# Queries turned ahead of the wait for the key sums, and the key sums of the first pairs from a ones product, in an attention and expert kernel

## The chip, the cores and the metric

The kernel runs on one core of a Trainium2 chip. The metric is the time of one execution on the device in microseconds. The engines are TensorE (PE in the rows, PEld for its weight loads), VectorE (DVE), ScalarE (ACT), GpSimd (POOL) and the DMA queues; SP is the queue of SyncE. Each engine works through its own instructions in the order of the program, and waits on semaphores for the others.

## What is computed

Multi-query attention over 8 batches, 16 heads, 384 positions and head size 64, with one key and value head per batch; its output, as 3072 rows of 1024, goes through a two-level mixture of 4 x 4 experts. All of it is float32 outside; the expert products run in bf16.

```python
scores = scale * np.matmul(q, k.transpose(0, 1, 3, 2))
attn = np.exp(scores - max) ; attn = attn / (sum(attn) + 1e-09)
x = np.matmul(attn, v)            # rows of 16 heads x 64
g_idx = argmax(x @ w_group) ; e_idx = argmax(xg @ w_expert[g])
out[token] = g_w * e_w * (relu(x @ w1[g, e]) @ w2[g, e])
```

## The kernel before

A batch has 16 x 384 query columns. They are cut into 6 chunks `g` of 2 x 512 columns (two heads' halves of the array at once), and two chunks make a pair `p`. So there are 24 pairs, three to a batch `b` (`r` is the pair's place in its batch). The queries arrive in a layout that VectorE's 32 x 32 turn brings into the form TensorE needs: `prep_q` (`qT`, line 176) for a pair of chunks, `prep_k` (`kT`, line 169) for a batch's keys.

The work of a pair:

- `scores(g, kt)`: for one of three blocks of 128 keys, two float32 matmuls of 64 rows each fill a PSUM tile `s` of 2 x 512 columns (line 185; two such tiles exist); ScalarE's exponential writes `pt` (line 187). No maximum is taken off.
- `pre_add` and `fold_keys`: VectorE adds the three `pt` blocks of a chunk in two steps (`presum`, lines 195 and 199), turns the sum in 32 x 32 blocks (`turn`, line 207) and sums along the row (`fold`, line 211). What is left of the sum over keys, 4 partition groups, a small product does in `invert`: `sm` (line 216), then a reciprocal `rc` (218) and a turn that spreads it over the partitions, `rinv` (220).
- `values(g)`: six matmuls of 64 output rows each into `o` (line 232). There is one buffer of `o`, and the gate's products `gps`, `lps` and `cps` take turns in it.
- `weigh(p)`: VectorE multiplies `o` by `rinv` into `xT` (240), which also frees `o`; GpSimd casts to bf16.

Pairs run one behind another: in step `p` the scores of pair `p` are made, and the values, the reciprocal and `xT` of pair `p - 1`. `manual_schedule` keeps the order in which the code is written. Up to pair 6 (`MOE_AT = 7`; `busy` is false) a step holds attention alone, and in some pairs the gate of the batch before: `gate_a` and `gate_b` at `r == 0` (product `gps`, copy, logits `lps`, arithmetic on VectorE with the exponential `ex`), `gate_c` at `r == 1` (counts `cps`, `cnt` at line 299, the choice of the batch's most used expert, and the DMA of its weights from GpSimd's queue). From pair 7 on, `fill(n)` puts `n` units of expert work (`hps`, line 329, and `yps`, line 338) at fixed places of each step. After the last pair follow the units that are left, and the tokens that went to other experts.

Queries are loaded from SyncE's queue three pairs ahead (`load_q(p + 3)` at the end of step `p`), behind `stats_q` on ScalarE, which reads the same buffer.

## Time and profile before

| | before |
|---|---|
| median of 3 runs | 570.04 us (569.46 to 573.44) |
| the profiled execution | 569.86 us, its span 567.9 us |
| TensorE busy | 496.1 us, 87% of the span |
| VectorE busy | 369.9 us, 65% |
| ScalarE busy | 242.0 us, 43% |
| GpSimd busy | 63.8 us, 11% |
| DMA | 73.06 MB, 129 GB/s on average |
| granted clock of TensorE, mean | 0.947 of full speed |

The span runs from the first to the last instruction. The chain of work that ended last lies on TensorE for 67% of the span and on VectorE for 22%. Busy shares are averages over stretches with different limits: the first pairs, the pairs with expert work, and the tail. The granted clock is given as a share of 2.4 GHz; 0.5 is the lower level, 1.2 GHz. A float32 matmul has two records in the trace, so a count there is twice that in the code.

### The profile page before, as it was taken

How to read it: one execution, taken by the hardware profiler on the slowest of the kernel's cores; microseconds unless marked ns; L12 is line 12 of the kernel's file. 1: busy time of each engine (PE TensorE's matmuls, PEld its weight loads, DVE VectorE, ACT ScalarE, POOL GpSimd, SP SyncE). 2: the span in 40 equal slices, each digit the busy share in tenths (PEclk: the TensorE clock that was granted, in tenths of full speed). 3: DMA queues.
4: the chain of work that ended last, by engine and by line, in shares of the span. 5: the costliest groups of instructions: out<-in, count | busy, mean ns of one | idle time of the engine just before them, and what ended most of it. 6: DMA issues, size and time to landing. Idle time of an engine off the chain costs nothing.

```text
span 567.9 us, 6824 instructions
## 1 busy us (share of the span) xinstructions
PE 496.1 (87%) x2521; PEld 210.1 (37%) x2521; DVE 369.9 (65%) x503; ACT 242.0 (43%) x342; POOL 63.8 (11%) x64
## 2 busy tenths in 40 slices
PE   6758677857979997999899998999899979989992
PEld 4222222313434342433443343434343434454550
DVE  2865776796979848775978496787788567241100
ACT  2434225233536444444634562556355435232331
POOL 0010011111011101110021002010111011010000
PEclk8798788879999998999999998999999989999997
DMA  9450223892359843986199529943697129689990
GB/s 122 44 67 0 38 70 47 136 213 74 59 72 216 213 96 43 199 176 160 39 165 201 171 47 143 208 154 85 99 210 176 46 45 206 176 189 236 237 253 16
DMA packets 148377, 73.06 MB, mean 129 GB/s; under 512 B 122587, under 2 KB 122587, under 8 KB 148336
## 3 DMA queue, kind: packets, MB, share of 16 engines
q0 software_dynamic: 19008, 37.84, 36.8%
q1 hardware_dynamic: 114928, 32.53, 27.1%
q10 hardware_dynamic: 14400, 2.16, 2.1%
q8 instruction: 23, 0.38, 0.3%
q14 instruction: 18, 0.15, 0.1%
HBM read 91.31 MB, written 19.40 MB: 195 GB/s over the span
## 4 chain that ended last, share of the span: by engine, by line
PE 67%; DVE 22%; issue 4%; DMA 2%; ACT 2%; SPq 1%; POOL 0%; DVEq 0%; POOLq 0%; ACTq 0%
PE o L232 23%; PE s L185 19%; PE yps L338 12%; PE hps L329 10%; DVE turn L207 4%; DVE presum L199 4%; DVE qT L176 3%; DVE presum L195 2%; DVE rinv L220 2%; DVE xT L240 2%; DMA out_dram<-y 2%; DVE fold L211 2%; PE gps L252 2%; ACT y L340 1%; DVE oh L278 1%
## 5 line engine op out<-in xcount | busy, mean ns | idle before, releaser
L187 ACT ACTIVATE pt<-s 128x1024 f32<-128x1024 f32 x144 | 140.1, 1020 | 175.0 <-PE s L185 174.9
L185 PE MATMUL s<-qT,kT 64*128 64x512 f32 x576 | 155.0, 659 | 35.6 <-DVE qT L176 17.6
L232 PE MATMUL o<-pt,v 128*64 128x512 f32 x576 | 139.8, 634 | 16.0 <-DVE cnt L299 16.0
L329 PE MATMUL hps<-xbf,w 128*128 128x384 bf16 x512 | 89.3, 326 | 2.2 <-ACT hT L331 0.9
L338 PE MATMUL yps<-w,hT 128*128 128x512 bf16 x384 | 89.5, 379 | 1.3 <-ACT y L340 1.3
L185 PEld LDWEIGHTS s<-qT,kT 64*128 64x128 f32 x576 | 53.7, 199 | 96.9 <-issue 79.6
L232 PEld LDWEIGHTS o<-pt,v 128*64 128x64 f32 x576 | 41.0, 145 | 115.3 <-issue 90.2
L195 DVE TENSOR_TENSOR presum<-pt 128x1024 f32<-128x1024 f32 x48 | 57.8, 1205 | 36.6 <-ACT pt L187 36.4
L241 POOL CAST xbf<-xT 128x1024 bf16<-128x1024 f32 x24 | 40.8, 1699 | 350.7 <-DVE xT L240 350.7
L329 PEld LDWEIGHTS <-w 128*128 128x128 bf16 x512 | 48.5, 99 | 48.1 <-issue 18.5
L207 DVE STREAM_TRANSPOSE turn<-presum 128x1024 f32<-128x1024 f32 x48 | 59.8, 1245 | 1.6
L199 DVE TENSOR_TENSOR presum<-presum,pt 128x1024 f32<-128x1024 f32 x48 | 58.6, 1221 | 2.9 <-DVE presum L195 0.5
L211 DVE TENSOR_REDUCE fold<-turn 128x32 f32<-128x1024 f32 x48 | 58.6, 1220 | 1.6
L218 DVE RECIPROCAL rc<-sm 128x32 f32<-128x32 f32 x24 | 8.6, 358 | 77.4 <-PE sm L216 77.4
L338 PEld LDWEIGHTS <-hT 128*128 128x128 bf16 x384 | 37.0, 100 | 51.9 <-issue 14.1
L340 ACT ACTIVATE y<-yps,gsel 128x512 f32<-128x512 f32 x48 | 32.9, 686 | 54.2 <-PE yps L338 49.3
L331 ACT ACTIVATE hT<-hps 128x384 bf16<-128x384 f32 x64 | 31.3, 490 | 40.2 <-PE hps L329 32.9
L176 DVE STREAM_TRANSPOSE qT<-qraw 128x1024 f32<-128x1024 f32 (+1 forms) x25 | 29.7, 1191 | 3.6 <-DMA qraw<-in_q_dram 3.6
L155 ACT ACTIVATE junk<-qraw 128x1024 bf16<-128x1024 f32 x24 | 25.2, 1052 | 14.5 <-DMA k<-in_k_dram 14.4
L220 DVE STREAM_TRANSPOSE rinv<-rc 128x1024 f32<-128x1024 f32 x24 | 29.9, 1245 | 0.8
L240 DVE TENSOR_TENSOR xT<-o,rinv 128x1024 f32<-128x1024 f32 x24 | 29.4, 1224 | 1.3
L93 POOL DMA_DIRECT2D w<-in_moe_w_dram x18 | 12.6, 706 | 101.3 <-DVE gsel L317 76.7
(123 smaller groups left out, 161.1 us busy)
## 6 DMA issues: line engine op xcount, KB each, us to landing
w<-in_moe_w_dram POOLq DMA_DIRECT2D x18, 1024.0 KB, 13.3
w<-in_moe_w_dram POOLq DMA_DIRECT2D x9, 2048.0 KB, 23.7
qraw<-in_q_dram SPq DMA_DIRECT2D x96, 128.0 KB, 3.8
out_dram<-y SPq DMA_DIRECT2D x48, 256.0 KB, 3.4
x_bf<-xbf SPq DMA_DIRECT2D x8, 768.0 KB, 3.4
k<-in_k_dram ACTq DMA_DIRECT2D x28, 48.0 KB, 2.2
v<-in_v_dram ACTq DMA_DIRECT2D x8, 96.0 KB, 2.6
xe<-x_bf SPq DMA_DIRECT2D x1, 768.0 KB, 9.5
```

The lines of the kernel that those rows point to most:

```text
L176: nc.vector.transpose(out=t[:, i * w:(i + 1) * w], in_=src[:, i * w:(i + 1) * w])
L185: nc.tensor.matmul(out=ps[:, par, :], lhsT=kT[b][r, kt * P:(kt + 1) * P], rhs=qT[g][r, :], start=True, stop=True)
L187: nc.scalar.activation(out=t[:], in_=ps[:], func=ACTF.Exp, scale=scale)
L195: nc.vector.tensor_add(out=t[:], in0=pt[g, 0][:], in1=pt[g, 1][:])
L199: nc.vector.tensor_add(out=t[:], in0=t[:], in1=pt[g, 2][:])
L207: nc.vector.transpose(out=t[:], in_=presum[g][:].rearrange("p a n -> p (a n)"))
L211: nc.vector.reduce_sum(out=fold[p][:, ch, :], in_=t[:].rearrange("p (b i) -> p b i", i=32), axis=AX)
L220: nc.vector.transpose(out=t[:].rearrange("p (b i) -> p b i", i=32), in_=rc[:].unsqueeze(2).to_broadcast([P, 32, 32]))
L232: nc.tensor.matmul(out=o_ps[p][64 * par:64 * par + 64, ch, :], lhsT=v_sb[b][:, kt, :], rhs=pt[g, kt][:, par, :], start=(kt == 0), stop=(kt ...
L241: nc.gpsimd.tensor_copy(out=xbf[b][:, cs], in_=xT[b][:, cs])
L329: nc.tensor.matmul(out=ps[:, 0:S], lhsT=w1[:, ko, fc * P:(fc + 1) * P], rhs=xb[:, ko * S:(ko + 1) * S], start=(ko == 0), stop=(ko == KO - 1))
L338: nc.tensor.matmul(out=ps[:], lhsT=state["h"][:, fo, st * P:(st + 1) * P], rhs=w2[:, fo, nh * CW:(nh + 1) * CW], start=(fo == 0), stop=(fo ...
```

## The change

Four things are changed.

- `prep_q(p + 1)` and `prep_k(b + 1)` are issued right after the first key addition of step `p`, ahead of `invert(p - 1)`. Before, they stood behind the first chunk's fold.
- For pairs 0 to 6, the turn and fold of the key sums on VectorE are gone. `sum_keys` puts four float32 matmuls (`kss`) with a block of ones of 32 columns on TensorE, one for each half of each chunk, at four column positions of one PSUM tile; VectorE turns that tile once (`krow`, 512 columns), and `invert` picks one column of each 32-block with four small matmuls instead of two. `presum` has three buffers instead of one.
- Two constants are built at the start (`ones32`, `selq`).
- With expert work, `gate_c` is issued ahead of the second chunk's additions and fold, instead of behind them and two units.

The diff, without a last hunk that gives three buffers to a tile of the fallback path:

```diff
@@ -135,6 +135,12 @@
     for a in range(2):
         nc.vector.tensor_copy(out=sel2[:, a, :], in_=sel[:])
 
+    ones32 = singles.tile([P, 32], FP32, name="ones32")
+    nc.vector.memset(ones32[:], 1.0)
+    selq = singles.tile([P, 4, 2, 32], FP32, name="selq")
+    for a in range(2):
+        nc.vector.tensor_copy(out=selq[:, :, a, :], in_=ident[:].rearrange("p (w j) -> p w j", w=4))
+
     gw = singles.tile([P, KO, 32], FP32, name="gw")
     nc.vector.memset(gw[:], 0.0)
 
@@ -191,7 +197,7 @@
 
     def pre_add(g, kt):
         if kt == 1:
-            t = pool.tile([P, 2, CW], FP32, tag="presum", bufs=1, name="presum")
+            t = pool.tile([P, 2, CW], FP32, tag="presum", bufs=3, name="presum")
             nc.vector.tensor_add(out=t[:], in0=pt[g, 0][:], in1=pt[g, 1][:])
             presum[g] = t
         elif kt == 2:
@@ -210,9 +216,25 @@
             fold[p] = pool.tile([P, 2, 32], FP32, tag="fold", name="fold")
         nc.vector.reduce_sum(out=fold[p][:, ch, :], in_=t[:].rearrange("p (b i) -> p b i", i=32), axis=AX)
 
+    key_rows = {}
+
+    def sum_keys(p):
+        ps = ps_m.tile([P, CW], FP32, tag="mm", name="kss")
+        for ch in range(2):
+            for par in range(2):
+                w = 2 * ch + par
+                nc.tensor.matmul(out=ps[32 * w:32 * w + 32, :], lhsT=ones32[:], rhs=presum[2 * p + ch][:, par, :], start=True, stop=True, tile_position=(0, 32 * w))
+        t = pool.tile([P, CW], FP32, tag="turn", bufs=1, name="krow")
+        nc.vector.transpose(out=t[:], in_=ps[:])
+        key_rows[p] = t
+
     def invert(p):
         sm = ps_m.tile([P, 32], FP32, tag="mm", name="sm")
-        for par in range(2):
+        if p in key_rows:
+            for ch in range(2):
+                for par in range(2):
+                    nc.tensor.matmul(out=sm[64 * par:64 * par + 64, 16 * ch:16 * ch + 16], lhsT=selq[:, 2 * ch + par].rearrange("p a j -> p (a j)"), rhs=key_rows[p][:].rearrange("p (b i) -> p b i", i=32)[:, :, 0], start=True, stop=True)
+        for par in range(0 if p in key_rows else 2):
             nc.tensor.matmul(out=sm[64 * par:64 * par + 64, :], lhsT=sel2[:].rearrange("p a b -> p (a b)"), rhs=fold[p][:, :, 16 * par:16 * par + 16], start=True, stop=True)
         rc = pool.tile([P, 32], FP32, tag="rc", name="rc")
         nc.vector.reciprocal(out=rc[:], in_=sm[:])
@@ -390,10 +412,16 @@
             scores(g, 0)
             scores(g, 1)
             pre_add(g, 1)
+            if p + 1 < NP:
+                prep_q(p + 1)
+            if r == 2 and b + 1 < B:
+                prep_k(b + 1)
         else:
             fill(2)
         if p > 0:
             values(g - 2)
+            if p - 1 < MOE_AT:
+                sum_keys(p - 1)
             if busy:
                 values(g - 1)
                 invert(p - 1)
@@ -410,17 +438,12 @@
         if not busy:
             if p < NP:
                 pre_add(g, 2)
-                fold_keys(g)
-            if p + 1 < NP:
-                prep_q(p + 1)
         elif p < NP:
             if r == 1:
                 gate_b(b - 1, between=True)
             fill(1)
             pre_add(g, 2)
             fold_keys(g)
-            if p + 1 < NP:
-                prep_q(p + 1)
             fill(1)
         if p < NP:
             scores(g + 1, 1)
@@ -431,11 +454,11 @@
             if p < NP:
                 pre_add(g + 1, 1)
                 pre_add(g + 1, 2)
-                fold_keys(g + 1)
+                if busy:
+                    fold_keys(g + 1)
 
         if not busy:
             if r == 2 and b + 1 < B:
-                prep_k(b + 1)
                 stats_k(b + 1)
             if r == 0 and 0 < b < B:
                 gate_a(b - 1)
@@ -444,8 +467,8 @@
                 gate_c(b - 1)
             fold_last()
         elif p < NP:
-            if r == 2 and b + 1 < B:
-                prep_k(b + 1)
+            if r == 1 and b > 0:
+                gate_c(b - 1)
             fold_last()
             fill(1)
             if r == 2 and b + 1 < B:
@@ -453,8 +476,6 @@
             fill(1)
             if r == 0 and 0 < b < B:
                 gate_a(b - 1)
-            if r == 1 and b > 0:
-                gate_c(b - 1)
             fill(p % 2)
             assert not inserts
         if r == 0 and b + 1 < B:
```

TensorE, the start of pair 1 to pair 3 (`s` scores, `o` values, `sm` the small product). Before:

```order
L185 MATMUL s<-qT,kT 128x512 x16
L232 MATMUL o<-pt,v 64x512 x6
L185 MATMUL s<-qT,kT 128x512 x4
L232 MATMUL o<-pt,v 64x512 x6
L216 MATMUL sm<-fold,sel_149 64x32 x2
L185 MATMUL s<-qT,kT 128x512 x8
```

After:

```order
L191 MATMUL s<-qT,kT 128x512 x16
L254 MATMUL o<-pt,v 64x512 x6
L226 MATMUL kss<-presum,ones_152 32x512 x4
L191 MATMUL s<-qT,kT 128x512 x4
L254 MATMUL o<-pt,v 64x512 x6
L236 MATMUL sm<-krow,selq 64x16 x4
L191 MATMUL s<-qT,kT 128x512 x8
```

Four `kss` matmuls have come in behind the first values, and `sm` has four instead of two; the rest stands as it did.

VectorE in the same place, from pair 1's end through pair 2's wait for `sm`. Before, starting with the turn of pair 2's queries:

```order
L176 STREAM_TRANSPOSE qT<-qraw 128x1024
L195 TENSOR_TENSOR presum<-pt 128x1024
L199 TENSOR_TENSOR presum<-presum,pt 128x1024
L207 STREAM_TRANSPOSE turn<-presum 128x1024
L211 TENSOR_REDUCE fold<-turn 128x32
L195 TENSOR_TENSOR presum<-pt 128x1024
L218 RECIPROCAL rc<-sm 128x32
L220 STREAM_TRANSPOSE rinv<-rc 128x1024
L240 TENSOR_TENSOR xT<-o,rinv 128x1024
L199 TENSOR_TENSOR presum<-presum,pt 128x1024
L207 STREAM_TRANSPOSE turn<-presum 128x1024
L211 TENSOR_REDUCE fold<-turn 128x32
```

After:

```order
L205 TENSOR_TENSOR presum<-presum,pt 128x1024
L201 TENSOR_TENSOR presum<-pt 128x1024
L205 TENSOR_TENSOR presum<-presum,pt 128x1024
L201 TENSOR_TENSOR presum<-pt 128x1024
L182 STREAM_TRANSPOSE qT<-qraw 128x1024
L175 STREAM_TRANSPOSE kT<-k 128x384
L228 STREAM_TRANSPOSE krow<-kss 128x512
L240 RECIPROCAL rc<-sm 128x32
L242 STREAM_TRANSPOSE rinv<-rc 128x1024
L262 TENSOR_TENSOR xT<-o,rinv 128x1024
L205 TENSOR_TENSOR presum<-presum,pt 128x1024
```

The turn of the queries has moved from behind `xT` and the fold to ahead of `rc`; turn and fold are gone, and the turn of `kss` has come in.

VectorE in pair 10 (expert work, `r == 1`), around `cnt`. Before:

```order
L199 TENSOR_TENSOR presum<-presum,pt 128x1024
L207 STREAM_TRANSPOSE turn<-presum 128x1024
L211 TENSOR_REDUCE fold<-turn 128x32
L176 STREAM_TRANSPOSE qT<-qraw 128x1024
L195 TENSOR_TENSOR presum<-pt 128x1024
L199 TENSOR_TENSOR presum<-presum,pt 128x1024
L207 STREAM_TRANSPOSE turn<-presum 128x1024
L211 TENSOR_REDUCE fold<-turn 128x32
L299 TENSOR_REDUCE cnt<-cps 128x16
```

After:

```order
L205 TENSOR_TENSOR presum<-presum,pt 128x1024
L213 STREAM_TRANSPOSE turn<-presum 128x1024
L217 TENSOR_REDUCE fold<-turn 128x32
L321 TENSOR_REDUCE cnt<-cps 128x16
```

Five instructions that stood ahead of `cnt` are now elsewhere: four follow the gate's arithmetic, and `qT` has been done ahead of `rc`.

## Rows read from the trace of the kernel before

**Rows 1.** Windows: stretch, length, then busy us of each engine, clock, DMA share, GB/s

```profile
0.00:140.37 140.37, 100.07 (x424) 37.35 (x424) 95.53 (x115) 52.06 (x64) 15.71 (x21) 0.84 0.53 82
140.37:482.75 342.38, 325.03 (x1640) 134.61 (x1642) 259.34 (x329) 166.44 (x238) 41.44 (x35) 0.99 0.68 134
482.75:567.90 85.15, 71.02 (x461) 38.13 (x460) 15.05 (x60) 23.55 (x40) 6.64 (x8) 0.97 0.80 185
```

**Rows 2.** Groups by line and form: busy us, mean ns, idle before, releasers

```profile
L185 PE MATMUL s<-qT,kT 64*128 64x512 f32 x576 | 155.0, 659 | 35.6 <-DVE qT L176 17.6 <-DVE kT L169 12.9 <-DVE cnt L299 4.7
L232 PE MATMUL o<-pt,v 128*64 128x512 f32 x576 | 139.8, 634 | 16.0 <-DVE cnt L299 16.0
```

**Rows 3.** Timeline of VectorE, pair 2: start us, length us, instruction, idle before

```profile
53.11 0.36 DVE L218 RECIPROCAL rc<-sm 128x32 f32<-128x32 f32 x1 [6.33 <-PE sm L216]
...
54.79 1.23 DVE L240 TENSOR_TENSOR xT<-o,rinv 128x1024 f32<-128x1024 f32 x1
55.93 1.22 DVE L199 TENSOR_TENSOR presum<-presum,pt 128x1024 f32<-128x1024 f32 x1
57.18 1.25 DVE L207 STREAM_TRANSPOSE turn<-presum 128x1024 f32<-128x1024 f32 x1
...
59.59 1.23 DVE L176 STREAM_TRANSPOSE qT<-qraw 128x1024 f32<-128x1024 f32 x1
```

**Rows 4.** Timeline of TensorE, pair 5 and the start of pair 6

```profile
105.24 2.80 PE L232 MATMUL o<-pt,v 128*64 128x512 f32 x12
...
112.51 0.26 PE L216 MATMUL sm<-fold,sel 128*64 128x32 f32 x4
112.69 1.99 PE L185 MATMUL s<-qT,kT 64*128 64x512 f32 x8
121.13 3.79 PE L185 MATMUL s<-qT,kT 64*128 64x512 f32 x8 [6.45 <-DVE kT L169]
```

**Rows 5.** Windows: first scores of pair 2; values behind a wait for `cnt`

```profile
40.68:44.46 3.78, 3.78 (x10) 1.30 (x12) 3.61 (x4) 1.02 (x1) 0.00 (x0) 0.50 0.16 13
...
223.36:230.45 7.09, 7.09 (x29) 2.33 (x29) 2.44 (x9) 0.00 (x0) 2.25 (x3) 0.76 0.56 86
```

**Rows 6.** Timeline of TensorE, last scores of pair 0, first of pair 1

```profile
16.46 1.13 PE L185 MATMUL s<-qT,kT 64*128 64x512 f32 x4 [0.20 <-ACT pt L187]
20.58 3.78 PE L185 MATMUL s<-qT,kT 64*128 64x512 f32 x8 [2.98 <-DVE qT L176]
```

**Rows 7.** Timeline of TensorE, gate of pair 3

```profile
76.73 1.50 PE L252 MATMUL gps<-xT,gw 128*32 128x384 f32 x16 [1.13 <-issue]
78.81 0.85 PE L261 MATMUL lps<-sel,part 128*128 128x32 f32 x6 [0.59 <-ACT part L254]
```

**Rows 8.** Timeline of VectorE: first instruction of the gate's arithmetic and the next addition

```profile
81.37 0.18 DVE L273 COPY L<-lps 128x60 f32<-128x60 f32 x1
...
83.37 1.22 DVE L195 TENSOR_TENSOR presum<-pt 128x1024 f32<-128x1024 f32 x1
...
101.71 0.17 DVE L299 TENSOR_REDUCE cnt<-cps 128x16 f32<-128x48 f32 x1
...
103.32 1.22 DVE L195 TENSOR_TENSOR presum<-pt 128x1024 f32<-128x1024 f32 x1
```

**Rows 9.** Timeline of ScalarE, from the gate's exponential to the next two of scores

```profile
82.22 0.25 ACT L282 ACTIVATE ex<-dl 128x60 f32<-128x60 f32 x1 [3.45 <-DVE dl L280]
...
85.82 1.92 ACT L187 ACTIVATE pt<-s 128x1024 f32<-128x1024 f32 x2
```

**Rows 10.** Timeline of TensorE, values behind a wait for `cnt`, first and last long one

```profile
223.36 7.07 PE L232 MATMUL o<-pt,v 128*64 128x512 f32 x24 [3.00 <-DVE cnt L299]
...
462.02 7.07 PE L232 MATMUL o<-pt,v 128*64 128x512 f32 x24 [3.00 <-DVE cnt L299]
```

**Rows 11.** DMA issues from 100 to 140 us: KB each, median us to landing

```profile
w<-in_moe_w_dram POOLq DMA_DIRECT2D x1, 2048.0 KB, 23.0
...
qraw<-in_q_dram SPq DMA_DIRECT2D x5, 128.0 KB, 11.2
```

More of the change, by code (lines that the diff above doesn't have):

```diff
@@ L657 @@
                 nc.vector.tensor_scalar(out=sm1[:, 1:2], in0=sm1[:, 0:1], scalar1=-scale, scalar2=None, op0=OP.mult)
-                at = pool.tile([P, S], FP32, tag="presum", bufs=1, name="at")
+                at = pool.tile([P, S], FP32, tag="presum", bufs=3, name="at")
                 nc.scalar.activation(out=at[:], in_=sp[:, 0, 0:S], func=ACTF.Exp, bias=sm1[:, 1:2], scale=scale)
```

## The prediction

> **What bounds the kernel now.** I first cut the span into three stretches by busy time [rows 1]: the first pairs (0 to 140.37 us, pairs 0 to 6, no expert work yet), the later pairs (to 482.75 us), and the tail. TensorE is busy 100.07 of 140.37 us in the first stretch and 325.03 of 342.38 us in the second, and its granted clock is 0.84 in the first against 0.99 in the second. So the first stretch has room on TensorE, the second only 17.35 us of it, and the question is what TensorE waits for.
>
> The groups of instructions by line say it [rows 2]: 35.6 us of idle time before the score matmuls, released by VectorE's turn of queries `qT`, turn of keys `kT` or the count `cnt` queued behind `qT`; and 16.0 us before the values matmuls, all released by `cnt`.
>
> VectorE's timeline in pair 2 shows why the scores wait [rows 3]. After 6.33 us of waiting for `sm`, it does `rc`, `rinv`, `xT`, the second key addition, a turn and a fold, and only then `qT` at 59.59. TensorE ran out of work meanwhile: in pair 5 its last scores start at 112.69, and the next at 121.13, after 6.45 us of idle time [rows 4]. Each engine waits for the other once per pair. The idle time also costs clock: the first scores after it ran at a granted 0.50 for 3.78 us [rows 5], where a block of the same eight records takes 1.99 us at the full clock [rows 4].
>
> **The change, first pairs.** `qT` moves into VectorE's wait for `sm` (6.33 us, so its 1.2 us are free there), and the two turns and two folds per pair go. In their place TensorE makes the key sums (`kss`) and VectorE turns 512 columns instead of 2 x 1024.
>
> Time 0 is the end of `sm`. TensorE's work in a pair, at full clock:
> - two score tiles, 1.99 us; then values, scores, values, `sm`: from 105.24 to 112.69 = 7.45 us; two more score tiles, 1.99 us [rows 4]. Sum 11.43.
> - The last two score tiles of a pair and the first two of the next now come in a row of four, with two PSUM buffers; within such a row in pair 0, TensorE waited 0.20 us for the exponential [rows 6]. I add 0.23.
> - `kss` is not in the trace. The nearest row is the gate's product, which also packs outputs of 32 columns at four column positions: 8 matmuls (16 records) of 384 columns in 1.50 us [rows 7]. Four of 512 columns: 1.50 x 4/8 x 512/384 = 1.0 us. The upper bound, if the four do not overlap: one costs at most the 1 us of a score tile's two matmuls, so 4 us. The lower bound is a quarter of that, the same 1.0. I take 1.0, since the gate's product has the same packing and type.
> - `sm` becomes four matmuls of 16 columns instead of two of 32. The two took 0.26 us [rows 4]; between 0 and twice that, I take 0.2 more.
>
> That makes 12.9 us for a pair without gate work.
>
> *A rule on the packing.* The gate rows give four column groups their whole factor of four. The Trainium skill, "TensorE: Matmul & The Clock Gate", Part 3 (Measured speedup vs the span model), measured 2.38 times for three column tiles, not three. By that, four reach 3.2, and `kss` would cost an estimated 1.25 us: 1.7 us more over seven pairs. The gate rows are this kernel's own, so the sum stays with 1.0.
>
> Does VectorE keep up? From [rows 3], `rc` starts 0.05 after `sm`, `xT` starts 1.68 after `rc` and ends at 2.95; the second addition for the first half ends at 4.1, then two additions for the second half, the last of them dependent, at pitches of 1.15 and 1.25, end at 6.5. TensorE needs `xT` (one buffer of `o`) when the next values start, at 1.99 + 1.99 + 0.23 = 4.2; and it needs the key sums at 4.2 + 2.7 = 6.9 for `kss`. So VectorE is early by 0.4 us: close to even, and TensorE sets the pace. Then VectorE does the first addition, `qT` and the turn of `kss` in TensorE's next 4.7 us (scores and values) before `sm`: about 0.65 us for the 512-column turn by half of the 1.25 between dependent VectorE steps.
>
> Pairs with gate work. In pairs 3 and 6, the gate's product must wait for `xT` at 3.0 (1.0 us after the scores), and product, copy and logits take from 76.73 to 79.66, or 2.93 us [rows 7]: logits end at 5.93 instead of scores at 1.99, and the wait in the row of four goes, so +3.7 and 16.6 us. VectorE's gate arithmetic takes 2.0 us [rows 8], and two additions follow to 10.4; `kss` is due at 5.93 + 1.99 + 2.7 = 10.6, so even. ScalarE gets from `ex` to the next exponentials in 3.6 us [rows 9] (key loads and statistics lie between); `ex` starts 0.85 after the logits are read [rows 8, 9], so they end at 5.95 + 0.85 + 3.6 + 1.92 = 12.3; scores that need their buffers start at 11.6 and 12.6, no wait. In pair 4, the count waits for `xT` and costs 1.2 us, and the gate's 1.6 us on VectorE [rows 8] make `kss` 0.3 us late: 12.9 + 1.3 = 14.2.
>
> Pair 1 starts when the scores of pair 0 end, 17.6, not at 20.58 [rows 6]. Pairs 1, 2, 5 at 12.9, pairs 3 and 6 at 16.6, pair 4 at 14.2: 86.1 us. Pair 7 then starts at 103.7 instead of 140.37: **36.7 us**. Of this about 3 us per pair is clock. The two constants built at the start (five rows of VectorE before the first load has landed) cost nothing; without that cover, under 1 us.
>
> **The change, later pairs.** `cnt` now stands ahead of the second half's two additions, turn and fold, and `qT` is gone from its front: about 6 us earlier. It ended TensorE's wait by 3.00 us [rows 10], so that wait goes. The turn and fold behind it are next needed by `sm`, after two score tiles and 5.3 us of values: covered. `qT` now stands ahead of `rc`, and may delay `rc` by its own 1.2 us; `rc`'s users, `xT` and then the next pair's values, are over 10 us of TensorE work away. So TensorE's 17.35 us of idle time in this stretch [rows 1] go. And where 3.00 us of idle time went ahead, three of six values blocks took 7.07 us, at 223.36 and 462.02 the first and last [rows 10]; the clock there was 0.76 [rows 5], so 7.09 x 0.76 = 5.39 at full: 1.7 us each, **5.1**. Against that, pair 7 pays for pair 6's `kss` and `sm` (1.2) and waits for its turn: the additions start only after the exponentials at 12.3, then `qT` and the turn end at 15.5, where TensorE is ready at 14.3: 1.2. Net 17.35 + 5.1 - 2.4 = **20.0 us**.
>
> The tail (85.15 us) has the same units in the same order: 0.
>
> Sum: 567.9 - 36.7 - 20.0 = 511.2 us of span. The profiled execution took 569.86, 1.96 more than its span, and the median is 570.04: **513 us**.
>
> **Rivals.**
> - *The clock does not hold* (0.10). Pauses remain: 1.0 and 0.6 us around the gate. If TensorE falls to 0.50 after these, each costs what it does now, 1.8 on scores and about 1.1 on values; in pairs 3 and 6 alone, 6 us (519); in all six, 18 us (531). Against: in pair 5 the pause before such a block was 6.45 us, and none of that length is left.
> - *`kss` does not overlap* (0.05): 3 us more in each of seven pairs, 534. Against: the gate's rows.
> - *The later gain is taken back* (0.07): `rc` behind `qT`, and weights asked for ahead of the queries' load instead of after it, turn half to all of the 20 us into other waits: 523 to 533. Against: VectorE's slack above.
> - *The tail eats it* (0.03): if weights set its end and arrive no sooner, up to 10 us, 523.
> - *Slower* (0.02): the early `qT` waits for its queries, and everything on VectorE waits behind it. The load is issued a pair and a half ahead, some 15 us; beside weights it took 11.2 us, and the weights 23.0 [rows 11]. From a landing of 15 us on it costs; 57 us would be lost if 23 pairs waited 2.5 us each, so if loads took over 17.5 us throughout: 575. For most pairs no weights are loading.
> - *No effect* (0.01): only if TensorE's wait were not for VectorE; the rows say it is.
>
> **Numbers.** The forecast has 0.72; its own range, from the roundings (1 us in each of six pairs, half of the 5 us of clock, 2 in the tail), is 505 to 521. For eight in ten I reach from 504 to 527, into the clock and give-back cases. A change of 1% is about what a measurement here can tell from none: faster 0.96, same 0.02, slower 0.02.
>
> **What would show it.** Right: TensorE's idle time before scores under 5 us in the whole span and none before values from `cnt`; a clock of 0.95 or more before pair 7; pair 7 starting near 104; `kss` near 1.0 us; a tail of 85 us. Wrong: `kss` at 3 us or more; a clock of 0.5 to 0.7 behind the gate's logits; `qT` waiting for its load; a new wait before `kss` on the additions, since VectorE's margin there is only 0.4 us.

## The result and the profile after

The changed kernel takes **520.86 us** (median; 520.51 to 521.16), beside 571.74 us for the kernel before on the same chip: a ratio of 0.911, 95% interval 0.906 to 0.916. The forecast was 513.0 us with a range of 504 to 527. The direction, the place and most of the size were right; 8 us of the gain that was forecast are missing. The profiled execution has a span of 519.0 us, where 511.2 had been worked out.

The windows of the changed kernel, cut at the same places as [rows 1] (pair 7's first scores, and the end of the last pair); the columns are as there:

```profile
0.00:105.51 105.51, 94.24 (x496) 34.62 (x496) 69.89 (x97) 51.03 (x64) 15.69 (x21) 0.98 0.69 103
105.51:432.68 327.17, 321.48 (x1651) 132.90 (x1651) 257.84 (x328) 165.92 (x238) 41.38 (x35) 1.00 0.74 143
432.68:519.00 86.32, 71.24 (x461) 38.25 (x460) 15.05 (x60) 23.41 (x40) 6.62 (x8) 0.95 0.77 178
```

Beside [rows 1], the first stretch is 34.9 us shorter (forecast 36.7), the later pairs 15.2 (forecast 20.0), and the tail 1.2 us longer (forecast 0). The three misses are 1.8, 4.8 and 1.2 us, 7.8 in all: the whole distance. The granted clock of the first pairs rose from 0.84 to 0.98.

The groups by line and form of the changed kernel, which answer to [rows 2], with two lines that are new among them (busy us, mean ns, then idle us before and its releasers):

```profile
L191 PE MATMUL s<-qT,kT 64*128 64x512 f32 x576 | 145.1, 622 | 5.3 <-DVE qT L182 3.5 <-ACT pt L193 1.8
L254 PE MATMUL o<-pt,v 128*64 128x512 f32 x576 | 130.4, 598 | 0.0
L360 PE MATMUL yps<-w,hT 128*128 128x512 bf16 x384 | 90.0, 379 | 5.4 <-DVE rc L240 4.2 <-ACT y L362 1.3
L182 DVE STREAM_TRANSPOSE qT<-qraw 128x1024 f32<-128x1024 f32 x23 | 28.5, 1240 | 27.4 <-DMA qraw<-in_q_dram 21.3 <-PE hps L351 6.1
```

The 35.6 us before the scores are down to 5.3, of which 3.5 are the first queries' own way in, there before as well. The 16.0 us before the values are gone. In their place stand 4.2 us before the expert product `yps`, ended by `rc`, and on VectorE 21.3 us in which `qT` waits for its load. These two lines are one story, told below.

The timeline of TensorE, changed kernel, from the `sm` of step 1 to that of step 2, with pair 2's first scores at 30.66 (start us, length us, instruction, idle before):

```profile
28.41 1.99 PE L191 MATMUL s<-qT,kT 64*128 64x512 f32 x8
30.66 2.04 PE L191 MATMUL s<-qT,kT 64*128 64x512 f32 x8 [0.27 <-ACT pt L193]
32.64 2.79 PE L254 MATMUL o<-pt,v 128*64 128x512 f32 x12
35.36 1.61 PE L226 MATMUL kss<-presum,ones 128*32 128x512 f32 x8
36.90 1.99 PE L191 MATMUL s<-qT,kT 64*128 64x512 f32 x8
38.82 2.79 PE L254 MATMUL o<-pt,v 128*64 128x512 f32 x12
41.44 0.36 PE L236 MATMUL sm<-krow,selq 128*64 128x16 f32 x8
```

TensorE runs through without a gap but for 0.27 us in the row of four score tiles (0.23 had been added). From `sm` to `sm` it is 13.32 us, 28.12 to 41.44; 12.9 had been forecast. Only `kss` is far off: 1.61 us, where 1.0 was wanted. The `kss` behind pair 3's gate, at 65.69, took 1.09.

### The profile page after: what moved, and what is told of

It is laid out like the page before. It is cut to its first block, busy times and chain, and to the rows that moved or that the text cites. A ratio compares the mean times of both kernels' runs of the same rounds, so it can differ in the third digit from the quotient of the medians.

```text
span 519.0 us, 6961 instructions
## 1 busy us (share of the span) xinstructions
PE 487.0 (94%) x2605; PEld 205.8 (40%) x2605; DVE 342.8 (66%) x485; ACT 240.4 (46%) x342; POOL 63.7 (12%) x64
## 4 chain that ended last, share of the span: by engine, by line
PE 61%; DMA 17%; SPq 7%; ACT 5%; DVE 5%; issue 3%; ACTq 1%; POOL 0%; POOLq 0%; DVEq 0%
PE s L191 17%; DMA qraw<-in_q_dram 14%; PE o L254 14%; PE yps L360 13%; PE hps L351 12%; SPq L78 7%; PE gps L274 2%; ACT pt L193 2%; DMA out_dram<-y 2%; DVE qT L182 2%; ACT junk L161 1%; PE kss L226 1%; ACT y L362 1%; DMA k<-in_k_dram 1%; PE lps L283 1%
## 5 line engine op out<-in xcount | busy, mean ns | idle before, releaser
L191 PE MATMUL s<-qT,kT 64*128 64x512 f32 x576 | 145.1, 622 | 5.3 <-DVE qT L182 3.5
L254 PE MATMUL o<-pt,v 128*64 128x512 f32 x576 | 130.4, 598 | 0.0
L201 DVE TENSOR_TENSOR presum<-pt 128x1024 f32<-128x1024 f32 x48 | 61.1, 1272 | 37.0 <-ACT pt L193 37.0
L191 PEld LDWEIGHTS s<-qT,kT 64*128 64x128 f32 x576 | 49.6, 188 | 64.8 <-issue 43.4
L254 PEld LDWEIGHTS o<-pt,v 128*64 128x64 f32 x576 | 38.6, 136 | 87.8 <-issue 74.9
L213 DVE STREAM_TRANSPOSE turn<-presum 128x1024 f32<-128x1024 f32 x34 | 42.4, 1246 | 1.2
L217 DVE TENSOR_REDUCE fold<-turn 128x32 f32<-128x1024 f32 x34 | 41.5, 1220 | 1.2
L161 ACT ACTIVATE junk<-qraw 128x1024 bf16<-128x1024 f32 x24 | 25.2, 1052 | 15.3 <-DMA k<-in_k_dram 15.2
```

What stands on the lines that cost most here:

```text
L191: nc.tensor.matmul(out=ps[:, par, :], lhsT=kT[b][r, kt * P:(kt + 1) * P], rhs=qT[g][r, :], start=True, stop=True)
L201: nc.vector.tensor_add(out=t[:], in0=pt[g, 0][:], in1=pt[g, 1][:])
L213: nc.vector.transpose(out=t[:], in_=presum[g][:].rearrange("p a n -> p (a n)"))
L217: nc.vector.reduce_sum(out=fold[p][:, ch, :], in_=t[:].rearrange("p (b i) -> p b i", i=32), axis=AX)
L254: nc.tensor.matmul(out=o_ps[p][64 * par:64 * par + 64, ch, :], lhsT=v_sb[b][:, kt, :], rhs=pt[g, kt][:, par, :], start=(kt == 0), stop=(kt ...
```

## The experiments

The experiments ran on three chips, each beside the kernel before, and a ratio is to that kernel on the same chip. Its medians were 570.10 us (the early turn, the key sums and the count alone, the clock's share), 572.69 (the cast, the changed kernel again, the key sums later, the queries earlier) and 574.76 (everything but the key sums, the key sums made twice, the best version).

### The early turn alone

The question was which of the four edits carries the gain. Kernel before, with the turn of queries and keys moved, and nothing else:

```diff
             pre_add(g, 1)
+            if p + 1 < NP:
+                prep_q(p + 1)
+            if r == 2 and b + 1 < B:
+                prep_k(b + 1)
...
-            if p + 1 < NP:
-                prep_q(p + 1)
```

> The kernel before with one part of the change: the turns of queries and keys stand ahead of the wait for the key sums, and everything else (turns and folds on VectorE in all pairs, the count behind them) stays. Theory A (the place of the turn of queries carries the first pairs' gain): VectorE's own work per pair, 13.9 us by its rows, then sets the pace instead of each engine waiting for the other at 20 us; pair 7 starts near 108 us instead of 140.4; with the count about 1.2 us sooner in the later pairs the time is near 532 us. Theory B (the removal of turns and folds carries it): pairs 1 to 6 keep most of their 20 us, pair 7 starts after 125 us, time 552 us or more.

Measured: 533.29 us (533.18 to 535.40), ratio 0.933 [0.928, 0.939]. Its profile has pair 7's first scores at 109.84 us instead of 140.37. So this one move brings 30.5 of the 34.9 us of the first stretch, with all turns and folds still on VectorE. What it leaves, in the waits of TensorE from 20 to 440 us (total, times, longest):

```profile
PE o L232 <- DVE cnt L299: 14.8, 7, 3.2
PE gps L252 <- DVE xT L240: 2.9, 1, 2.9
PE gps L252 <- issue: 2.9, 1, 2.9
PE sm L216 <- DVE fold L211: 2.4, 2, 1.2
```

The count still holds up the values; and twice `sm` waits 1.2 us for the fold, and the gate's product 2.9 us instead of about 1.1, since VectorE is now late by its turns and folds.

### The key sums alone

The changed kernel with the early turns and `gate_c` put back:

```diff
-            if p + 1 < NP:
-                prep_q(p + 1)
-            if r == 2 and b + 1 < B:
-                prep_k(b + 1)
...
                 pre_add(g, 2)
+            if p + 1 < NP:
+                prep_q(p + 1)
```

> The kernel before with the other part alone: key sums of pairs 0 to 6 by the ones product on TensorE, and the turns of queries and keys and the count at their old places. Theory A: the scores still wait for the turn of queries, though with one turn and one fold less in front: about 3.3 us of idle time per pair instead of 6, so 16 us a pair at the full clock; pair 7 starts near 116 us, or near 125 us if the clock still falls in the shorter pauses; time 546 to 555 us. Theory B: close to the whole gain of the first pairs, pair 7 near 108 us, time 538 us.

Measured: 555.32 us (554.88 to 555.80), ratio 0.971 [0.965, 0.976]; pair 7 starts at 123.69. Timeline of TensorE, this kernel, pair 2:

```profile
28.52 1.99 PE L191 MATMUL s<-qT,kT 64*128 64x512 f32 x8
33.97 3.55 PE L191 MATMUL s<-qT,kT 64*128 64x512 f32 x8 [3.46 <-DVE qT L182]
```

With fewer instructions ahead of it, `qT` comes earlier, but TensorE still waits 3.46 us for it, and the scores behind the pause still run slowly, 3.55 us for a block that takes 1.99. Shortening VectorE's chain is worth 16.7 us here; taking the turn out of it is worth 30.5. The two are not added up: they remove the same wait.

### The count alone

Kernel before, with `gate_c` ahead of the second half's additions:

```diff
+            if r == 1 and b > 0:
+                gate_c(b - 1)
             fold_last()
...
-            if r == 1 and b > 0:
-                gate_c(b - 1)
             fill(p % 2)
```

> The kernel before with the third part alone: in pairs with expert work the count stands ahead of the second chunk's additions, turn and fold. Theory: TensorE's six waits of 16.0 us in all before the values go, and with them the three long values blocks (5.1 us of clock), nothing else changes: first stretch 140 us as before, time near 549 us. Rival (the wait comes back at another place, since VectorE still has the same work): 557 us or more, with new idle time before the scores or the small product sm.

Measured: 549.26 us (548.43 to 554.12), ratio 0.962 [0.956, 0.968]. The group of values matmuls in this kernel:

```profile
L232 PE MATMUL o<-pt,v 128*64 128x512 f32 x576 | 134.9, 615 | 0.0
```

No wait of the values for the count is left, where [rows 2] had 16.0 us, and no values block of 7.07 us as in [rows 10]. The median is 20.8 us below that of the kernel before; the wait (16.0) and the slow blocks behind it (5.1) had been put at 21.1.

### Everything but the key sums

The two moves together, turns and folds of the first pairs still on VectorE:

```diff
             if p < NP:
                 pre_add(g, 2)
+                fold_keys(g)
...
-            if p - 1 < MOE_AT:
-                sum_keys(p - 1)
```

> The changed kernel without its key sums on TensorE: turns and folds stay on VectorE in all pairs, while the queries' turn and the count stand early. Theory (the key sums add 4 us in the first pairs on top of the early turn): pair 7 starts near 110 us instead of 105.5, the later pairs as in the changed kernel, 524 us. Rival (the early turn alone does it, and the rest is given back later to the queries' loads): 521 us.

Measured: 525.11 us (524.76 to 526.28), ratio 0.915 [0.910, 0.920]. So the product with ones, the part of the change with most new code, is worth 4 to 5 us (medians 525.11 and 520.68, on two chips; spans 524.3 and 519.2). And the count, worth 20.8 us alone, adds only 7.4 us of span to the early turn (531.7 to 524.3; by the medians 8.2). The waits for `cnt` went from 14.8 to 1.7 us, but `yps` now waits 4.6 us for `rc`, where the kernel with the early turn alone has no such wait:

```profile
L185 PE MATMUL s<-qT,kT 64*128 64x512 f32 x576 | 147.3, 631 | 7.0 <-DVE qT L176 4.6 <-ACT pt L187 1.8 <-DVE kT L169 0.6
L232 PE MATMUL o<-pt,v 128*64 128x512 f32 x576 | 131.3, 602 | 2.7 <-DVE cnt L299 1.7 <-DVE xT L240 1.0
L338 PE MATMUL yps<-w,hT 128*128 128x512 bf16 x384 | 90.1, 379 | 5.9 <-DVE rc L218 4.6 <-ACT y L340 1.3
```

The 1.1 us more before the scores belong to the kernel's first queries (4.6 us against 3.5) and moved the first scores by only 0.2 us. The clock took another part of the missing gain, 2.4 us in the last two of the rows below. Timeline of TensorE in this execution, the gate of pair 6 and pair 7's first scores:

```profile
106.14 2.56 PE L252 MATMUL gps<-xT,gw 128*32 128x384 f32 x16 [2.93 <-DVE xT L240]
109.27 1.49 PE L261 MATMUL lps<-sel,part 128*128 128x32 f32 x6 [0.57 <-ACT part L254]
110.69 3.79 PE L185 MATMUL s<-qT,kT 64*128 64x512 f32 x8
```

The granted clock was 0.50 over the last two rows. With the early turn alone, the same pause of 2.93 us slowed the gate's product as well (2.79 us, at a clock of 0.53), but the logits took 0.85 us and the scores 1.99, at 1.00. This execution was the longest of the four (526.28 us; the others 524.76 to 525.30).

The new wait for `rc` needs both moves. With the early turn alone, VectorE never waited for queries in the later pairs: the first ones were asked for at 131.32 us, ahead of the weights at 135.06, and landed in 3.3 (median of four). With the count alone, queries were asked for beside the weights and landed up to 25.6 us later, but `qT` stood late enough in VectorE's order not to wait for them. Together, an early `qT` meets a late load.

### The clock's share

To part the pause itself from the clock it costs, the kernel before got work of no use in the pause: 90 small bf16 products, ahead of the last fold in the steps of pairs 0, 1, 2, 4 and 5. `qT` comes no earlier by it.

```diff
+        if not busy and (r != 0 or b == 0):
+            hot = ps_m.tile([P, CW], FP32, tag="mm", name="hot")
+            for _ in range(90):
+                nc.tensor.matmul(out=hot[:, 0:P], lhsT=ones_bf[:], rhs=ones_bf[:], start=True, stop=True)
```

> The kernel before, with 90 small bf16 matmuls on constants (their result is read by nobody) in TensorE's idle time of pairs 0, 1, 2, 4 and 5, to tell the clock's share from the wait's. They take about 5 us of 6 us of idle time. Theory (half of the first pairs' gain beyond the wait itself is clock: first scores 3.78 instead of 1.99 us, first values 3.7 to 4.0 instead of 2.8): the first stretch gets about 2.8 us shorter in each of the four or five pairs behind such a pause, pair 7 starts near 128 us, time near 557 us. Rival (the slow scores and values come from their operands, not from the pause): no change, 570 us.

Measured: 559.89 us (558.65 to 561.80), ratio 0.979 [0.973, 0.985]. Timeline of TensorE, this kernel:

```profile
34.74 5.20 PE L433 MATMUL hot<-ones_bf 128*128 128x128 bf16 x90
40.80 1.99 PE L185 MATMUL s<-qT,kT 64*128 64x512 f32 x8 [0.86 <-DVE qT L176]
```

The scores still wait for `qT`, but take 1.99 us instead of the 3.78 of [rows 5], and pair 7 starts at 130.02: 10.4 us earlier. That is the clock's share, 2.1 us for each of five pauses. The forecast had put it at about 3 us a pair; the sum did not rest on that, since it was built up from full-clock blocks.

### The key sums made twice

If `kss` is on the path and its four column groups run side by side, a second set must cost about 1 us per pair; if they ran one behind another, about 4; if VectorE set the pace, pair 7 would start at most 2 us later.

```diff
         ps = ps_m.tile([P, CW], FP32, tag="mm", name="kss")
-        for ch in range(2):
+        for rep in range(2):
+          for ch in range(2):
```

> The changed kernel with the key-sum products of pairs 0 to 6 made twice into the same place (the second time is extra work): 1.0 us more on TensorE in each of seven steps. Theory (TensorE paces the first pairs, with VectorE behind it by half a microsecond in three or four of them): 1.0 us more in three steps, 0.5 us more in the steps where the first product now waits; pair 7 starts 4 to 5 us later, time 525 us. Rival (VectorE paces them): pair 7 at most 2 us later, 522 us. If the products did not overlap among the column positions, each set would cost 3 to 4 us more: 545 us.

Measured: 526.72 us (525.90 to 527.44), ratio 0.919 [0.913, 0.924]. Timeline of TensorE, this kernel, pairs 1 and 2:

```profile
22.48 1.92 PE L227 MATMUL kss<-presum,ones 128*32 128x512 f32 x16
...
36.12 2.46 PE L227 MATMUL kss<-presum,ones 128*32 128x512 f32 x16
```

Two sets take 1.92 us where one takes 1.06, so the second costs 0.86: they overlap, and TensorE sets the pace. The 0.54 us by which the second row is longer did not go away: VectorE's chain starts at `sm`, and `kss` stands at the same distance behind `sm` as before. The gate's last logits of pair 6 start at 109.37 instead of 104.72, 4.65 us later; the span is 3.3 us longer and the time 6.0, so part of that difference lies outside the span, and why stays open.

### The cast on another engine

In steps 1, 2 and 5 of the changed kernel one addition takes 2.06 us instead of 1.22, and the `kss` that needs it, the first of the next step, comes late. GpSimd's cast of `xT` runs at that moment. Here the casts of these steps go to ScalarE:

```diff
-        nc.gpsimd.tensor_copy(out=xbf[b][:, cs], in_=xT[b][:, cs])
+        if p in (0, 1, 4):
+            later.append(lambda: nc.scalar.copy(out=xbf[b][:, cs], in_=xT[b][:, cs]))
+        else:
+            nc.gpsimd.tensor_copy(out=xbf[b][:, cs], in_=xT[b][:, cs])
...
             stats_q(p)
+            while later:
+                later.pop(0)()
```

> The changed kernel with the cast of pairs 0, 1 and 4 (made in steps 1, 2 and 5) moved from GpSimd to ScalarE, behind the step's statistics. Theory (the second chunk's first addition takes 2.06 instead of 1.22 us there because GpSimd's cast, which the addition before it held up, reads the same memory at that time, and VectorE waits until it is done): 1.22 us in those steps, key-sum products back to about 1.06 us, 1.6 us less in all, 519.2 us. Rival (the additions wait for the exponentials that write their inputs at that time, or for TensorE): the additions stay at 2.06 us and the time at 520.9 us.

Timeline of VectorE, changed kernel, end of step 1:

```profile
30.20 1.22 DVE L262 TENSOR_TENSOR xT<-o,rinv 128x1024 f32<-128x1024 f32 x1
31.34 1.22 DVE L205 TENSOR_TENSOR presum<-presum,pt 128x1024 f32<-128x1024 f32 x1
32.47 2.06 DVE L201 TENSOR_TENSOR presum<-pt 128x1024 f32<-128x1024 f32 x1
34.63 1.23 DVE L205 TENSOR_TENSOR presum<-presum,pt 128x1024 f32<-128x1024 f32 x1
```

Timeline of GpSimd, changed kernel, same place:

```profile
31.49 1.96 POOL L263 CAST xbf<-xT 128x1024 bf16<-128x1024 f32 x1 [29.22 <-DVE xT L262]
```

Timeline of VectorE with the cast on ScalarE:

```profile
32.07 1.22 DVE L205 TENSOR_TENSOR presum<-presum,pt 128x1024 f32<-128x1024 f32 x1
33.20 1.22 DVE L201 TENSOR_TENSOR presum<-pt 128x1024 f32<-128x1024 f32 x1
34.52 1.23 DVE L205 TENSOR_TENSOR presum<-presum,pt 128x1024 f32<-128x1024 f32 x1
```

The addition is back at 1.22 us, and from the first `kss` to the start of pair 6's last logits it takes 80.52 us instead of 82.13, as expected. But the time stayed: 520.75 us (520.23 to 522.66), ratio 0.910 [0.906, 0.915], against 520.68 and 0.909 for the changed kernel again on the same chip. Of the 1.6 us, about 1.0 was given back between pair 7's first scores and the last gate product: `yps` waits 4.5 us for `rc` (4.1), and `sm` in pair 7 1.9 us for `krow` (1.4). The rest does not show as a gain in the profiled executions because the first `kss` itself stands 0.4 us later there (23.31 against 22.91) and the tail is 0.3 us longer; no run tells whether that has to do with the cast.

### The changed kernel again, and the key sums later

The changed kernel once more, as the measure for its neighbours:

> The changed kernel as it stands, once more on the chip of the next three, to compare them with: 520.9 us as before, with slow additions of 2.06 us in pairs 1, 2 and 5, key-sum products of 1.61 us there, and 4.2 us of waits before the expert products for the buffer that rc reads.

Measured: 520.68 us (519.55 to 521.63), ratio 0.909 [0.905, 0.913].

The other way to test the late `kss` is to ask for it later on TensorE, behind one block of scores more:

```diff
             values(g - 2)
-            if p - 1 < MOE_AT:
+            if busy and p - 1 < MOE_AT:
                 sum_keys(p - 1)
...
             if not busy:
+                sum_keys(p - 1)
                 values(g - 1)
```

> The changed kernel with the key-sum products of pairs 0 to 5 moved behind the next two score tiles on TensorE, 2 us later, with the cast left on GpSimd. Theory (the products of 1.61 us hold a wait of 0.55 us for the last addition; the margin of VectorE there was set too high by the slow addition): products back to 1.06 us with additions still at 2.06 us, 1.6 to 2.0 us less, 519 us. Rival (the products take longer by themselves, beside what VectorE reads): 1.61 us stays, 521 us; if the small product sm then waits for the turn of the key sums, up to 3 us more.

Timeline of TensorE, this kernel, pair 2:

```profile
35.96 1.99 PE L191 MATMUL s<-qT,kT 64*128 64x512 f32 x8
37.87 1.06 PE L226 MATMUL kss<-presum,ones 128*32 128x512 f32 x8
38.87 2.80 PE L254 MATMUL o<-pt,v 128*64 128x512 f32 x12
41.50 0.36 PE L236 MATMUL sm<-krow,selq 128*64 128x16 f32 x8
```

`kss` takes its 1.06 us though the cast is still on GpSimd, and from `sm` to `sm` it is 12.79 us (28.71 to 41.50): the 0.55 us were a wait for the addition, hidden inside a matmul row. The row merges eight records: in the changed kernel the last four start at 35.92, 0.56 us behind the first, and VectorE's last addition ends at 35.86. The time again stayed, 520.92 us (519.40 to 522.38), ratio 0.910 [0.906, 0.914]: the stretch with pair 3's gate, from the `sm` of step 3 to that of step 4, got 1.0 us longer (17.88 against 16.89), where the scores now wait 1.29 us for the exponential instead of 0.28, and pair 7 starts at 105.00 instead of 105.51. `sm` in pair 7 then waits 1.6 us for `krow` instead of 1.4.

### The queries asked for earlier

Neither of these moved the time, and `yps` waited for `rc` in both, 4.5 and 4.2 us. So the load itself was next. In the changed kernel the queries are asked for at the end of a step, behind the batch's weights. Here they are asked for ahead of them, early in the step, with the statistics that read the buffer:

```diff
                 prep_k(b + 1)
+            stats_q(p)
+            if p + 3 < NP:
+                load_q(p + 3)
...
-        if p < NP:
-            stats_q(p)
-            if p + 3 < NP:
-                load_q(p + 3)
```

> The changed kernel with the statistics and the load of queries three pairs ahead issued early in each step (behind the turn of the next queries) instead of at its end, so that the loads land most of a step sooner and stand ahead of the weights' loads. Theory (the four waits of 4.2 us before expert products come from the turn of queries, which stands ahead of rc and waits for its load; VectorE waits 21 us for such loads in the later pairs): these waits shrink to 1 us or less, and the time to near 517 us. Rival (rc is late because of VectorE's own work ahead of it): the waits stay, 521 us; the statistics now ahead of the exponentials could cost up to 1 us more.

Measured: 514.54 us (514.30 to 515.00), ratio 0.898 [0.895, 0.902]: 6.1 us better, 2 more than expected. The group of `qT` in this kernel, and TensorE's waits from 107 to 434 us:

```profile
L182 DVE STREAM_TRANSPOSE qT<-qraw 128x1024 f32<-128x1024 f32 x23 | 28.5, 1238 | 0.0
```

```profile
PE sm L236 <- DVE krow L228: 1.0, 1, 1.0
PE lps L283 <- issue: 0.5, 3, 0.2
PE yps L360 <- issue: 0.3, 2, 0.2
```

`qT` no longer waits, and neither does `yps` for `rc`. That is the cause of most of the second miss, shown by taking it away.

### The best version

With the loads early, the cast's 1.6 us should stay. First the cast alone on top:

> The version with early statistics and loads, and the cast of steps 1, 2 and 5 on ScalarE as well. Alone, the cast saved 1.6 us up to pair 7 and lost 1.0 us of it again to the waits behind the turn of queries. Theory (the queries' loads, which land when the weights beside them do, gave it back): with the loads early the 1.6 us now stay but for the 0.4 us at pair 7, 513.3 us. Rival (something else in the later pairs sets their end): 514.5 us as without the cast.

Measured: 512.49 us (511.81 to 512.95), ratio 0.893 [0.889, 0.897], 2.0 us below the kernel with the early queries. Then also the keys' and values' loads on SyncE's queue, since ScalarE, which issued them, was late with the exponentials of pair 6:

```diff
-                (nc.sync if b == 0 else nc.scalar).dma_start(out=kt[64 * a + 32 * j:64 * a + 32 * j + 32], in_=kv[b, 0, j])
+                nc.sync.dma_start(out=kt[64 * a + 32 * j:64 * a + 32 * j + 32], in_=kv[b, 0, j])
...
-        nc.scalar.dma_start(out=vt[:], in_=v[b, 0].rearrange("(st p) d -> p st d", st=ST))
+        (nc.scalar if b == 0 else nc.sync).dma_start(out=vt[:], in_=v[b, 0].rearrange("(st p) d -> p st d", st=ST))
```

> The same, and the keys and values of the next batch asked for from SyncE's queue instead of ScalarE's. The 2.4 us that ScalarE spends on issuing them stand ahead of the exponentials that pair 4 and pair 7 begin with. Theory (the wait of 1.0 to 1.9 us for the turned key sums in pair 7 comes from these exponentials): that wait goes, and the 0.3 us before scores in pair 4; 511.8 us. Rival (VectorE's own work is what is late there): the wait stays, 513.3 us; keys behind queries on SyncE's queue could come late and cost a few us.

Measured: **511.46 us** (510.92 to 511.96), ratio 0.891 [0.888, 0.895]. Timeline of TensorE, changed kernel, pair 7:

```profile
115.39 0.41 PE L236 MATMUL sm<-krow,selq 128*64 128x16 f32 x8 [1.42 <-DVE krow L228]
```

and of this kernel:

```profile
112.64 0.36 PE L236 MATMUL sm<-krow,selq 128*64 128x16 f32 x8
```

The wait for `krow` is gone. This kernel is the fastest of all here: 9 us below the changed one.

## Why the prediction was right, and where it was off

**What bounds the kernel: right.** TensorE waited for VectorE's turn of the queries in the first pairs and for `cnt` later. The early turn alone brought 30.5 us of the first stretch; the count alone brought 20.8 us, where its two rows gave 21.1. All three stretches missed to the same side, so the time is not near by errors that cancel. Yet of the four signs that the prediction named for being wrong, two came: a wait before `kss` on the additions, and `qT` waiting for its load.

**The cost of `kss`: right.** Taken as 1.0 us from [rows 7], measured 1.06, and 0.86 for a second set. The estimate beside it had drawn on the Trainium skill, "TensorE: Matmul & The Clock Gate", Part 3 (Measured speedup vs the span model), and came to 1.25 us. The measurement decides: this kernel's own rows were the better source, and four column groups here gave nearly their whole factor. `sm` took 0.36 us where about 0.46 had been allowed.

**The clock: right.** It holds at 0.98 over the first stretch in spite of the pauses around the gate (1.13 and 0.59 us in pair 3); the rival in which it does not hold is out for these pauses. Behind the pauses of 2.9 us in the kernel without key sums on TensorE it did come true, once.

**"Does VectorE keep up? ... early by 0.4 us": the first step that failed.** TensorE does set the pace, as the doubled `kss` shows, but VectorE is late by 0.55 us in steps 1, 2 and 5, and by 0.47 in step 4 (`kss` took 1.53 us; 0.3 forecast). The sum priced the additions at pitches of 1.15 and 1.25 us from [rows 3]. There, the second addition is followed by a turn, which reads one operand; after the change it is followed by another addition, which reads two, and GpSimd's cast is under way just then. The addition takes 2.06 us. The two experiments agree on the place (the cast taken away, the product asked for later). The three waits cost 1.6 us, which is what taking the cast away gave back; what else was mis-sized is small and has both signs (`sm` 0.1 us cheaper a step, the stretch with pair 3's gate 16.89 us against 16.6, that with pair 4's count 14.20 as forecast). The prediction had named this wait as what would prove it wrong, but not its cause.

The trace of before held a hint that was not used. Timeline of GpSimd, kernel before, casts in a first pair and in a later one:

```profile
135.56 1.97 POOL L241 CAST xbf<-xT 128x1024 bf16<-128x1024 f32 x1 [17.82 <-DVE xT L240]
151.33 1.04 POOL L241 CAST xbf<-xT 128x1024 bf16<-128x1024 f32 x1 [13.80 <-DVE xT L240]
```

The same cast takes 1.04 us or 1.97. The long one starts with an addition of VectorE's under way and ends when it would if it had waited for that. The Trainium skill, "SBUF — State Buffer", section "Who interferes with whom", states that a VectorE instruction with two SBUF inputs contends with a GpSimd instruction that reads SBUF, at a port pair that only one of them can hold at a time. The traces agree: the cast's 1.96 us exceed 1.04 by 0.92, the addition's 2.06 exceed 1.22 by 0.84, and without the cast on GpSimd the addition takes 1.22.

**"`rc`'s users, `xT` and then the next pair's values, are over 10 us of TensorE work away": the second step that failed.** It left out what `rc` frees. `sm`, which `rc` reads, sits in one of the two PSUM buffers that the expert products `hps` and `yps` also take (line 68; lines 232, 349 and 358). As long as `rc` has not run, `yps` has one buffer too few. The rival *slower* had the chain right, an early `qT` that waits for its queries with everything on VectorE behind it, and priced it too low at a chance of 0.02, because it asked only whether it could make the kernel slower. Its numbers were off as well. Timelines of VectorE and TensorE, changed kernel:

```profile
153.89 1.25 DVE L182 STREAM_TRANSPOSE qT<-qraw 128x1024 f32<-128x1024 f32 x1 [5.27 <-DMA qraw<-in_q_dram]
155.06 0.32 DVE L240 RECIPROCAL rc<-sm 128x32 f32<-128x32 f32 x1
```

```profile
155.43 1.89 PE L360 MATMUL yps<-w,hT 128*128 128x512 bf16 x8 [0.60 <-DVE rc L240]
383.39 1.89 PE L360 MATMUL yps<-w,hT 128*128 128x512 bf16 x8 [1.61 <-DVE rc L240]
```

`yps` waits four times in all; for the last of these waits the profile names `hps` as what released `qT`, at 381.85; with the queries early that wait went too. VectorE was ready for `qT` at 148.6 us and got the queries at 153.9. They had been asked for from 128.38 on, so the slack was 20 us, not the 15 of the forecast; but the load took longer still, since the weights stood ahead of it. Issues on GpSimd's and SyncE's queues, changed kernel, then the DMA issues from 128 to 140 us:

```profile
126.73 1.37 POOL L93 DMA_DIRECT2D w<-in_moe_w_dram  x2 [6.81 <-DVE gm L337]
128.38 20.00 SPq L78 DMA_DIRECT2D qraw<-in_q_dram  x4
```

```profile
qraw<-in_q_dram SPq DMA_DIRECT2D x3, 128.0 KB, 22.8
```

The 22.8 us are the median of the first three of four loads (15.8, 23.9 and 22.8); the fourth was asked for only at 141.1 us and landed in 11.9.

The prediction had taken 11.2 us from [rows 11], a median over five issues. In the kernel before, the queries of the same pair were asked for at 160.44 us, ahead of the weights at 165.30, and landed in 3.8 (median of four). With the count earlier, the order turned round; the rival *the later gain is taken back* said so, and came true for a quarter of the 20 us.

**The later pairs in numbers.** TensorE is idle 5.69 us there (327.17 less 321.48), of which `rc` is 4.2 and `krow` 1.4; 1.2 had been forecast, all of it `krow`. Busy time fell by 3.55 us against 3.9 (5.1 less the 1.2 of `kss` and `sm`). So the idle time is the miss. The price of `krow` was right, and its reason too: with the loads taken off ScalarE's queue it went.

**The tail: 1.2 us longer, open.** From the last gate product to the end it takes 76.3 us in the kernel before and 77.4 in the changed one; over the other kernels it lies between 75.8 and 77.5. The two traces place the difference: TensorE's rows agree to 0.01 us until 58.5 us behind that product, and only then ScalarE's last `y` starts later, at 60.2 us instead of 59.3, behind a wait for an earlier output's DMA. Why that DMA landed later stays open; no run was made for it.

**What a local saving is worth.** Taking the cast away saved 1.6 us in the first pairs and nothing in the time, as long as the queries came late; with the queries early, it gained 2.0 us.

## What to carry to other kernels

Moving an instruction into a wait of its own engine can be worth more than making the chain around that wait shorter, since the pause that is left still costs clock; here the move did most of the work. But two moves that each cost nothing alone can make a new wait together: for each instruction that is moved ahead, list every reader and every buffer that it holds up, PSUM included, and ask which DMA is now asked for in another order. When two-operand additions of VectorE are put side by side, look at what GpSimd reads at the time: the cost shows as a longer instruction and not as idle time.

## What the runs showed of the hardware

- An addition of two operands on VectorE and a cast on GpSimd don't run side by side: 2.06 us instead of 1.22, and 1.96 instead of 1.04. A turn of one operand beside the cast kept its 1.25 us.
- A row of merged matmuls can hold a wait: the blocks of `kss` lasted 1.61 us with no idle time shown before them, and 1.06 us when their operand was early.
- Loads of 128 KB of queries landed in 3.8 us when asked for 4.9 us ahead of 4 MB of weights, and in 15.8 to 23.9 us when asked for 1.7 to 3.4 us behind them. Asking for the queries earlier in the step, ahead of the weights, was worth 6 us of the kernel's time.
- A pause of 2.9 us before the gate's product of pair 6 cost clock: the product took 2.6 to 2.8 us at 0.53 to 0.55, against 1.50 us behind a pause of 1.2 us.
- The kernel before, with its pauses, ran between 567.67 and 576.47 us over the three chips of the experiments, a spread of 1.5%, its granted clock between 0.935 and 0.952; the changed kernel, nearly without pauses, lay between 519.55 and 521.63 us, or 0.4%.
